# One output tile stored row by row through a single transfer, five stores cut in two: attention, then a channel mix

## The chip, the core and the metric

The kernel runs on one core of a Trainium2 chip. The core has a matmul engine (TensorE, PE in the profile; PEld is its loading of weights), a vector engine (VectorE, DVE), an activation engine (ScalarE, ACT), GpSimd (POOL) and SyncE (SP). Each engine runs its own list of instructions in order, and engines wait for each other by semaphores. Data move between memory (HBM) and the on-chip buffer (SBUF) by DMA; SP, ACT and POOL can issue transfers. Matmul results land in eight PSUM banks. The metric is the device time of one execution in microseconds (us).

## The reference

The first half is an attention through 32 memory slots for 8 batches, 8 heads, 576 tokens and head width 64; the second is a channel mix over the result, `x` of 8 x 576 tokens and 512 features:

```python
a = softmax(phi)                      # over the 32 slots
k_m, v_m = a^T k, a^T v               # per batch and head
x = softmax(q k_m^T / 8) v_m          # -> x[b, s, 512]
x_prev = x moved on by one token, zero at s = 0
xk = mu_k * x + (1 - mu_k) * x_prev   # and xr with mu_r
out = sigmoid(xr w_r) * (max(xk w_k, 0)^2 w_v)
```

`w_k` is 512 x 1024, `w_v` 1024 x 512, `w_r` 512 x 512. The output is float32, 8 x 576 rows of 512.

## The kernel before

**Tokens in blocks of 64.** A batch's 576 tokens are taken as 64 rows p by NJ = 9 positions j, token = 9p + j, and are kept in the order j first (from batch 1 on with j = 0 last): a block is the 64 tokens of one j. In this order the previous token's block is simply the block before. An output tile t is 128 places, that is two blocks of 64; there are 36 tiles. One block's rows lie nine rows apart in the output. Two neighbouring blocks j and j + 1 of one batch are, for each p, two adjacent rows in the output.

**Stages.** Per batch, attention steps give normalised weights (`atn`) and slot values (`vb`). From batch 1 on the rest goes by chunks of 512 places: chunk step `x8:v` makes x for chunk 8 with matmuls, `x8:d0d` and `x8:d2d` the difference to the token before (two feature blocks of 128 each), and the four mixes `x8:k0d`, `x8:k2d`, `x8:r0d`, `x8:r2d` scale the difference by mu (line 563) and add x (line 568), which writes xk or xr into a ring. The ring `xkT` (and `xrT`) is 128 partitions x 4 feature blocks x 2304 columns, bf16; a place's column is its number modulo 2304. The last block of each batch is written by an add of its own (line 572).

**What reads the rings.** A key step such as `c7:3` (chunk 7, hidden block 3) does four matmuls over the four feature blocks of `xkT` (line 611), then a relu on ACT (line 615) and a square on ACT or DVE (lines 621, 623) into `sq`. A gate step `g:28` (tile 28) does four matmuls from `xrT` (line 644) and a tanh on ACT (line 647). A value step `o:31` does eight matmuls from `sq` (line 665); DVE combines them with the gate into one of four `o` buffers (line 673) and the rows are stored. For the last four tiles a value step can be cut into halves of 256 columns: `o:33b` and `o:33a`.

**What sets the order.** Nothing is scheduled: the order is written out by hand in the strings of `PLAN`, and every engine gets its instructions in that order. The layer below places the semaphore waits from what each instruction reads and writes. Around the change the plan reads

```python
"c6:5 7:y1 g:26 x7:vm g:25 g:27 x7:d0d x7:d2d x7:k0d x7:r2e x8:v o:24 x7:k2d o:25 o:26 o:27 x8:d0d x7:r0e c7:1",
"c7:6s x8:d2d x8:k0d c7:3s c7:7s g:29 x8:k2d c7:5 c7:4 g:31 c8:1 c8:5s c7:0 c7:2 g:30 x8:r0d c8:0s c8:4 c8:2",
"x8:r2d o:31 c8:7 g:28 c8:3s g:32 c8:6s o:28 o:30 g:35 g:33 o:29 o:32 o:33b g:34 o:35 o:34 o:33a",
```

Chunk 7 is places 3648 to 4159, ring columns 1344 to 1855; chunk 8 is places 4160 to 4607, columns 1856 to 2303.

**Stores.** Each tile is stored by two transfers, one for each block of 64 rows (line 599): both from SP, but for the last four tiles the second block from ACT. A transfer raises one of eight completion counts; SP's and ACT's transfers take the eight in turn, in the order in which they are written. At the end of the program SP passes one wait for each count, in a fixed order, before the engines meet and the execution ends.

Of the kernel before, what the change touches and what calls it, by code (L numbers as in the profile page):

```python
# [53 lines left out]

NJ = 9
SG = 4
RL = 3
HALF_ROOT = 0.5 ** 0.5

# [2 lines left out]
def kernel(  # L62
# [13 lines left out]
    nc = tc.nc  # L76
    B, H, S, D = q.shape
# [8 lines left out]
    QR = S // NJ  # L86
# [15 lines left out]
    def bank():  # L102
        return f"ps{next(banks)}"
# [96 lines left out]
    for g in range(4):  # L200
        r = slice(g * M, (g + 1) * M)
# [34 lines left out]
    def turn(name, n):  # L236
        turns[name] = turns.get(name, -1) + 1
        return f"{name}{turns[name] % n}"
# [3 lines left out]
    def head_tiles(pss, st, src, lo, hi, cols=slice(0, None), **flags):  # L242
        for c in range(2):
            for g in range(HH):
                r = slice(g * M, (g + 1) * M)
                nc.tensor.matmul(pss[g][c * D:(c + 1) * D, cols], lhsT=src[r, c], rhs=st["at"][r, c, lo:hi],  # L246
                                 skip_group_check=True, **flags)
# [264 lines left out]
    def chunk_x(c):  # L512

        lo = (c - 1) * CT
        hi = min(lo + CT, TOK)
        n, plain = hi - lo, min(hi, TOK - QR) - lo
        ends = [b * S - QR for b in range(1, B) if lo <= b * S - QR < hi]

        def tile_x():
            if c not in xs:  # L520
                xs[c] = work.tile([128, ND, QR + CT], BF16, name="x", tag=f"x{c % 3}")
            return xs[c]

        def values(c0, c1, both=False):

            def go():
                x = tile_x()
                if c > 1:
                    nc.vector.tensor_copy(x[:, :, :QR], xs[c - 1][:, :, CT:])
                pss = [psum.tile([128, CT], F32, name="nops", tag=bank())[:, :c1 - c0] for _ in range(ND)]  # L530
                for b in range(1, B):
                    g0, g1 = max(lo + c0, (b - 1) * S), min(lo + c1, b * S)
                    if g0 < g1:
                        head_tiles(pss, states[b], states[b]["vb"], g0 - (b - 1) * S, g1 - (b - 1) * S,
                                   slice(g0 - lo - c0, g1 - lo - c0), start=True, stop=True)
                for i in range(ND):
                    (nc.vector.tensor_copy if both and i % 2 else nc.scalar.copy)(x[:, i, c0:c1], pss[i])  # L537
            return go

        def diff(pr, m):  # L540

            def go():
                if c not in ds:
                    ds[c] = work.tile([128, ND, CT], BF16, name="diff", tag=f"diff{c % 2}")
                x, d = xs[c][:, pr:pr + m], ds[c][:, pr:pr + m]
                nc.vector.tensor_sub(d[:, :, :plain], x[:, :, QR:QR + plain], x[:, :, :plain])  # L546
                for e in ends:
                    e -= lo
                    first = xs[c - 1][:, pr:pr + m, e:e + QR]
                    nc.vector.tensor_sub(d[:, :, e + 1:e + QR], first[:, :, 1:], x[:, :, e:e + QR - 1])  # L550
                    nc.vector.tensor_copy(d[:, :, e:e + 1], first[:, :, :1])  # L551
            return go

        def mix(which, pr, m, by_act=False):
            def go():
                ring = (xk_T, xr_T)[which][:, pr:pr + m]
                t = work.tile([128, 2, CT], BF16, name="mu_d", tag=turn("mu_d", 2))[:, :m]
                for i in range(m):
                    o = which * ND + pr + i
                    if by_act:  # L560
                        nc.scalar.activation(t[:, i, :n], ds[c][:, pr + i, :n], AF.Copy, scale=mu1[:, o:o + 1])  # L561
                    else:
                        nc.vector.tensor_scalar_mul(t[:, i, :n], ds[c][:, pr + i, :n], mu1[:, o:o + 1])
                x = xs[c][:, pr:pr + m]
                cut = -(S + lo) % RING
                for p0, p1 in ((0, cut), (cut, plain)) if 0 < cut < plain else ((0, plain),):
                    g = (S + lo + p0) % RING
                    nc.vector.tensor_add(ring[:, :, g:g + p1 - p0], x[:, :, QR + p0:QR + p1], t[:, :, p0:p1])  # L568
                for e in ends:
                    e -= lo  # L570
                    g = (S + lo + e) % RING
                    nc.vector.tensor_add(ring[:, :, g:g + QR], xs[c - 1][:, pr:pr + m, e:e + QR], t[:, :, e:e + QR])
            return go
        return values, diff, mix
# [17 lines left out]


    def store(o, t, cols):
        for n in range(2):
            b, r = divmod(t * 128 + n * QR, S)
            j = (r // QR + 1) % NJ if b else r // QR
            eng = nc.scalar if n and t >= NTOK // 128 - 4 else nc.sync
            eng.dma_start(out=out[b].rearrange("(p j) d -> p j d", j=NJ)[:, j, cols], in_=o[n * QR:(n + 1) * QR, cols])

    def keys(c):
        start = STARTS[c]
# [2 lines left out]
        def key(fi, lo, hi, by_act=False):  # L605
            def go():
                pk = psum.tile([128, CT], F32, name="pk", tag=bank())[:, :hi - lo]
                cut = min(hi, -(lo + 1) // RING * -RING)
                for p0, p1 in ((lo, cut), (cut, hi)) if cut < hi else ((lo, hi),):
                    for di in range(ND):  # L610
                        nc.tensor.matmul(pk[:, p0 - lo:p1 - lo], lhsT=wk_sb[:, di, fi * 128:(fi + 1) * 128],  # L611
                                         rhs=xk_T[:, di, p0 % RING:p0 % RING + p1 - p0],
                                         start=(di == 0), stop=(di == ND - 1))
                rl = work.tile([128, CT], BF16, name="rl", tag=turn("rl", RL))[:, :hi - lo]
                nc.scalar.activation(rl, pk, AF.Relu, scale=HALF_ROOT)  # L615
# [15 lines left out]
    gated, outs, homes, parts = {}, {}, {}, {}  # L631
    free = {"sg": list(range(SG)), "o": list(range(4))}

# [18 lines left out]
    def value(t, hs=((0, 1),), n=1, f0=0, f1=NF):  # L652

        def go():
            p = t * 128 % (2 * S)
            for h0, h1 in hs:
                cols = slice(h0 * Dm // n, h1 * Dm // n)
                pv = opened.get(t) if f1 - f0 < NF else None
                fresh = pv is None
                if fresh:  # L660
                    pv = psum.tile([128, Dm], F32, name="pv", tag=bank())
                if f1 - f0 < NF:
                    opened[t] = pv
                for fi in range(f0, f1):
                    nc.tensor.matmul(pv[:, cols], lhsT=sq[:, fi, p:p + 128], rhs=wv_sb[:, fi, cols],  # L665
                                     start=(fi == 0 and fresh), stop=(fi == NF - 1),
                                     skip_group_check=f1 - f0 < NF)
                if f1 < NF:
                    continue
                if t not in outs:  # L670
                    outs[t] = take("o", t)
                o = outs[t]
                nc.vector.scalar_tensor_tensor(o[:, cols], in0=gated[t][:, cols], scalar=1.0, in1=pv[:, cols],  # L673
                                               op0=AL.add, op1=AL.mult)
                store(o, t, cols)
                parts[t] = parts.get(t, 0) + Dm * (h1 - h0) // n
            if parts.get(t) == Dm:
                for name in free:
                    free[name].append(homes[name, t])
        return go  # L680
# [19 lines left out]
    for n, word in enumerate(" ".join(PLAN).split()):  # L700
        who, _, name = word.partition(":")
# [40 lines left out]
```

## Time and profile before

| | us |
|---|---|
| median of 3 runs | 200.18 (199.85 to 200.54) |
| the profiled execution, its own time | 199.63 |
| its span, first to last instruction | 197.9 |
| PE busy | 189.6 (96%) |
| DVE busy | 158.3 (80%) |
| ACT busy | 146.9 (74%) |
| POOL busy | 31.0 (16%) |
| mean granted TensorE clock, share of full | 0.988 |

The profile is of one execution, and times in it count from the start of its span. A row of the timeline gives the start, the busy time, the engine, the line of the kernel, the operation, out<-in, the shapes and how many such instructions it merges; in square brackets stands how long the engine was idle before and what ended that. The chain of waits follows the work that ended last back from the end; in order of time each row is start, length, engine, tile and line. A row of a group gives the count, the busy time, the mean of one in ns and the idle time before. A window's row gives the busy time of each engine in it, the granted clock (PEclk; 1.00 is full) and the DMA share.

### The profile page before, as it was taken

What the parts mean: (1) busy time and instruction counts of PE and PEld (TensorE: products, weight loads), DVE (VectorE), ACT (ScalarE), POOL (GpSimd) and SP (SyncE); (2) the same over time, 40 slices, a digit from 0 to 9 for tenths busy, and PEclk for the clock granted to TensorE, in tenths of its full rate; (3) what the DMA queues carried; (4) which work ended last, traced back from release to release, by engine and by line L of the source; (5) the groups of instructions that cost most, each with busy time, mean ns of one, the idle gap of its engine ahead of it and who ended that gap; (6) DMA issues with size and microseconds to landing.
All of it is one profiled execution on the core that took longest, in us unless ns stands there. A gap on an engine that the chain in (4) does not pass through costs nothing.

```text
span 197.9 us, 5488 instructions
## 1 busy us (share of the span) xinstructions
PE 189.6 (96%) x2182; PEld 96.7 (49%) x2205; DVE 158.3 (80%) x440; ACT 146.9 (74%) x302; POOL 31.0 (16%) x47
## 2 busy tenths in 40 slices
PE   7988999999999999999999999999999999999991
PEld 2534665765454445445357645444443444444550
DVE  6079869899979998999999999999996997452232
ACT  2338779696989998899998978897699759854210
POOL 7824333412040040004700000000000000000000
PEclk9979999999999999999999999999999999999998
DMA  6999999999999999955999953232240063012444
GB/s 164 189 263 212 205 207 198 266 224 279 239 280 228 221 304 205 215 117 151 217 234 279 251 101 79 57 83 53 66 96 3 2 146 68 0 29 48 98 123 130
DMA packets 24554, 31.30 MB, mean 158 GB/s; under 512 B 1992, under 2 KB 19664, under 8 KB 24528
## 3 DMA queue, kind: packets, MB, share of 16 engines
q0 software_dynamic: 17424, 20.91, 56.6%
q1 hardware_dynamic: 6176, 8.92, 17.9%
q10 hardware_dynamic: 928, 1.11, 1.7%
q8 instruction: 17, 0.28, 0.6%
q14 instruction: 9, 0.07, 0.1%
HBM read 38.28 MB, written 9.44 MB: 241 GB/s over the span
## 4 chain that ended last, share of the span: by engine, by line
PE 82%; DMA 9%; POOL 4%; ACT 1%; issue 1%; DVE 1%; POOLq 0%
PE pk L611 30%; PE pv L665 30%; PE pr L644 16%; DMA wk<-in_moe_w_k_dram 9%; PE kvps L280 4%; PE nops L246 2%; PE scps L372 1%; POOL q L183 1%; POOL kvs L126 1%; ACT x L537 1%; ACT mu_d L561 1%; POOL kvs L129 1%; POOL ph L122 0%; POOL wk L167 0%; DVE diff L546 0%
## 5 line engine op out<-in xcount | busy, mean ns | idle before, releaser
L611 PE MATMUL pk<-xkT,wk 128*128 128x512 bf16 (+4 forms) x345 | 67.5, 340 | 0.6 <-DMA wk<-in_moe_w_k_dram 0.2
L665 PE MATMUL pv<-wv,sq 128*128 128x512 bf16 (+1 forms) x321 | 65.6, 353 | 0.3
L615 ACT ACTIVATE rl<-pk 128x512 bf16<-128x512 f32 (+3 forms) x80 | 42.9, 554 | 10.9 <-PE pk L611 10.3
L611 PEld LDWEIGHTS <-wk 128*128 128x128 bf16 x352 | 33.0, 98 | 28.5 <-issue 1.1
L665 PEld LDWEIGHTS <-sq 128*128 128x128 bf16 x328 | 31.3, 98 | 30.0 <-issue 0.8
L644 PE MATMUL pr<-wr,xrT 128*128 128x512 bf16 x135 | 34.7, 379 | 0.6 <-issue 0.2
L673 DVE SCALAR_TENSOR_TENSOR o<-sg,pv 128x512 f32<-128x512 f32 (+1 forms) x41 | 24.3, 613 | 13.3 <-PE pv L665 12.2
L647 ACT ACTIVATE sg<-pr 128x512 f32<-128x512 f32 x36 | 20.9, 601 | 9.7 <-PE pr L644 9.5
L561 ACT ACTIVATE mu_d<-diff,mu 128x512 bf16<-128x512 bf16 x34 | 22.4, 717 | 3.6 <-DVE diff L551 2.1
L623 DVE TENSOR_TENSOR sq<-rl 128x192 bf16<-128x192 bf16 (+5 forms) x66 | 18.9, 319 | 7.7 <-ACT rl L615 7.0
L644 PEld LDWEIGHTS <-xrT 128*128 128x128 bf16 x144 | 13.5, 98 | 15.5 <-issue 0.7
L621 ACT ACTIVATE sq<-rl 128x512 bf16<-128x512 bf16 (+5 forms) x38 | 19.8, 535 | 1.0
L537 ACT CAST x<-nops 128x512 bf16<-128x512 f32 (+3 forms) x32 | 15.1, 560 | 4.0 <-PE nops L246 4.0
L357 DVE STREAM_TRANSPOSE qT<-q 128x576 uint32<-128x576 uint32 x16 | 11.8, 755 | 2.3 <-DMA q<-in_q_dram 2.3
L432 DVE TENSOR_TENSOR atn<-e,lz 128x256 bf16<-128x256 bf16 (+1 forms) x32 | 13.0, 445 | 0.1
L377 ACT ACTIVATE e<-scps 128x288 bf16<-128x288 f32 x32 | 10.5, 416 | 3.4 <-PE scps L372 3.4
L546 DVE TENSOR_TENSOR diff<-x 128x1024 bf16<-128x1024 bf16 (+1 forms) x16 | 10.7, 671 | 1.9 <-ACT x L537 1.6
L423 DVE STREAM_TRANSPOSE lz<-se 128x256 f32<-128x256 f32 (+2 forms) x24 | 12.0, 527 | 0.1
L216 PE MATMUL idle<-zeros 128*128 128x512 bf16 (+1 forms) x35 | 10.7, 466 | 1.0 <-DVE zeros L144 1.0
L414 DVE TENSOR_REDUCE se<-eT 128x18 f32<-128x576 bf16 (+3 forms) x17 | 11.2, 659 | 0.2
L266 ACT ACTIVATE em<-ph 128x1152 bf16<-128x1152 f32 (+1 forms) x9 | 9.4, 1053 | 2.6 <-DMA ph<-in_phi_dram 2.6
L568 DVE TENSOR_TENSOR xrT<-x,mu_d 128x1024 bf16<-128x1024 bf16 (+3 forms) x18 | 10.9, 613 | 0.5 <-ACT mu_d L561 0.2
(72 smaller groups left out, 152.6 us busy)
## 6 DMA issues: line engine op xcount, KB each, us to landing
out_dram<-o SPq DMA_DIRECT2D x59, 128.0 KB, 2.4
kvs<-in_v_dram POOLq DMA_DIRECT2D x8, 576.0 KB, 14.2
ph<-in_phi_dram POOLq DMA_DIRECT2D x7, 576.0 KB, 13.1
kvs<-in_k_dram POOLq DMA_DIRECT2D x7, 576.0 KB, 15.8
q<-in_q_dram POOLq DMA_DIRECT2D x6, 576.0 KB, 16.8
q<-in_q_dram POOLq DMA_DIRECT2D x4, 288.0 KB, 10.4
out_dram<-o SPq DMA_DIRECT2D x18, 64.0 KB, 5.3
wk<-in_moe_w_k_dram POOLq DMA_DIRECT2D x2, 512.0 KB, 15.2
```

The source lines that it names most:

```text
L423: nc.vector.transpose(st["lz"].rearrange("p c (b t h) -> p (c b) h t", t=PB, h=2)[:, b0:b0 + n], st["se"][:, b0:b0 + n].unsqueeze(3).to_br ...
L432: nc.vector.tensor_mul(st["at"][:, c, sl], st["e"][:, c, sl], st["lz"][:, c, sl])
L537: (nc.vector.tensor_copy if both and i % 2 else nc.scalar.copy)(x[:, i, c0:c1], pss[i])
L561: nc.scalar.activation(t[:, i, :n], ds[c][:, pr + i, :n], AF.Copy, scale=mu1[:, o:o + 1])
L611: nc.tensor.matmul(pk[:, p0 - lo:p1 - lo], lhsT=wk_sb[:, di, fi * 128:(fi + 1) * 128], rhs=xk_T[:, di, p0 % RING:p0 % RING + p1 - p0], sta ...
L615: nc.scalar.activation(rl, pk, AF.Relu, scale=HALF_ROOT)
L621: nc.scalar.activation(sq[:, fi, p:p + p1 - p0], rl[:, part], AF.Square)
L623: nc.vector.tensor_mul(sq[:, fi, p:p + p1 - p0], rl[:, part], rl[:, part])
L644: nc.tensor.matmul(pr, lhsT=xr_T[:, di, c0:c0 + 128], rhs=wr_sb[:, di, :], start=(di == 0), stop=(di == ND - 1))
L647: nc.scalar.activation(gated[t], pr, AF.Tanh, scale=0.5)
L665: nc.tensor.matmul(pv[:, cols], lhsT=sq[:, fi, p:p + 128], rhs=wv_sb[:, fi, cols], start=(fi == 0 and fresh), stop=(fi == NF - 1), skip_gr ...
L673: nc.vector.scalar_tensor_tensor(o[:, cols], in0=gated[t][:, cols], scalar=1.0, in1=pv[:, cols], op0=AL.add, op1=AL.mult)
```

## The change

Tile 33 is places 4224 to 4351, ring columns 1920 to 2047, two neighbouring blocks of one batch. The changed kernel keeps these 128 places in another order: the two blocks are interleaved, so that place 2p + n of the tile holds row p of block n. All mixes that write these columns are cut in three adds: the 64 columns before the tile, the tile's 128 with a step of two columns in the write, and the 192 after. Only chunk 8 has them, so four mixes are touched. Everything that follows works on the tile's places in whatever order they stand; only the store must know it. It becomes, for each half of the columns, one transfer of 128 rows from SP, in place of one of 64 rows from SP and one of 64 from ACT. Apart from that, for tiles 20, 22, 23, 25 and 26 the first block's transfer is cut into two of 256 columns each, both from SP.

```diff
+SPLIT = (20, 22, 23, 25, 26)
+PAIRED = 33
...
                 cut = -(S + lo) % RING
-                for p0, p1 in ((0, cut), (cut, plain)) if 0 < cut < plain else ((0, plain),):
+                pair = PAIRED * 128 - S - lo
+                pieces = ((0, cut), (cut, plain)) if 0 < cut < plain else ((0, plain),)
+                if 0 < pair < plain:
+                    pieces = ((0, pair), (pair, pair + 128), (pair + 128, plain))
+                for p0, p1 in pieces:
                     g = (S + lo + p0) % RING
-                    nc.vector.tensor_add(ring[:, :, g:g + p1 - p0], x[:, :, QR + p0:QR + p1], t[:, :, p0:p1])
+                    to, a0, a1 = ring[:, :, g:g + p1 - p0], x[:, :, QR + p0:QR + p1], t[:, :, p0:p1]
+                    if p0 == pair:
+                        to = to.rearrange("k c (p n) -> k c n p", n=2)
+                        a0, a1 = (a.rearrange("k c (n p) -> k c n p", n=2) for a in (a0, a1))
+                    nc.vector.tensor_add(to, a0, a1)
...
     def store(o, t, cols):
-        for n in range(2):
-            b, r = divmod(t * 128 + n * QR, S)
-            j = (r // QR + 1) % NJ if b else r // QR
+        at = [(b, (r // QR + 1) % NJ if b else r // QR) for b, r in
+              (divmod(t * 128 + n * QR, S) for n in range(2))]
+        if t == PAIRED:
+            (b, j), _ = at
+            nc.sync.dma_start(out=out[b].rearrange("(p j) d -> p j d", j=NJ)[:, j:j + 2, cols], in_=o[:, cols])
+            return
+        for n, (b, j) in enumerate(at):
             eng = nc.scalar if n and t >= NTOK // 128 - 4 else nc.sync
-            eng.dma_start(out=out[b].rearrange("(p j) d -> p j d", j=NJ)[:, j, cols], in_=o[n * QR:(n + 1) * QR, cols])
+            mid = (cols.start + cols.stop) // 2
+            for c in (slice(cols.start, mid), slice(mid, cols.stop)) if t in SPLIT and n == 0 else (cols,):
+                eng.dma_start(out=out[b].rearrange("(p j) d -> p j d", j=NJ)[:, j, c], in_=o[n * QR:(n + 1) * QR, c])
```

## The prediction

> **What bounds the kernel now.** I read the head of the page and the chain of waits, then the chain in order of time and the timeline where the change acts, then the last microseconds.
>
> ```profile
> span 197.9 us, 5488 instructions
> PE 189.6 (96%) x2182; PEld 96.7 (49%) x2205; DVE 158.3 (80%) x440; ACT 146.9 (74%) x302; POOL 31.0 (16%) x47
> PE 82%; DMA 9%; POOL 4%; ACT 1%; issue 1%; DVE 1%; POOLq 0%
> ```
> ```profile
> 157.96 1.94 PE pv L665 x9
> 159.90 3.45 PE pk L611 x16
> 163.35 0.86 PE pr L644 x4
> 164.21 1.08 PE pk L611 x5
> ...
> 166.80 3.24 PE pk L611 x16
> ...
> 177.28 0.86 PE pr L644 x4
> ...
> 193.61 0.02 issue
> 193.63 0.42 DVE o L673
> ```
>
> TensorE (PE) is the bound: from 157.96 to 193.61 the chain is matmuls without a hole but for a few 0.05 us of issue. Whatever stops PE here moves the end by as much; what VectorE (DVE) and SyncE (SP) do costs nothing until PE waits for it. The changed adds stand in this stretch:
>
> ```profile
> 159.74 3.62 PE L611 MATMUL pk<-xkT,wk 128*128 128x512 bf16 x16
> 162.55 0.42 DVE L623 TENSOR_TENSOR sq<-rl 128x512 bf16<-128x512 bf16 x1
> 162.88 0.55 DVE L546 TENSOR_TENSOR diff<-x 128x768 bf16<-128x768 bf16 x1
> 163.56 0.57 DVE L563 TENSOR_SCALAR mu_d<-diff,mu 128x448 bf16<-128x448 bf16 x2
> 164.17 0.56 DVE L568 TENSOR_TENSOR xkT<-x,mu_d 128x768 bf16<-128x768 bf16 x1
> 164.64 0.22 DVE L572 TENSOR_TENSOR xkT<-x,mu_d 128x128 bf16<-128x128 bf16 x1
> 164.78 0.57 DVE L563 TENSOR_SCALAR mu_d<-diff,mu 128x448 bf16<-128x448 bf16 x2
> 165.39 0.56 DVE L568 TENSOR_TENSOR xkT<-x,mu_d 128x768 bf16<-128x768 bf16 x1
> 165.86 0.22 DVE L572 TENSOR_TENSOR xkT<-x,mu_d 128x128 bf16<-128x128 bf16 x1
> ```
>
> The 16 matmuls from 159.74 are the steps c7:1, c7:6, c7:3, c7:7, four each, 3.45/16 = 0.216 us apart; the 164.17 add is x8:k0d, the 165.39 add x8:k2d. PE is some 2.7 us ahead of DVE here (c7:3's first at 159.74 + 8 x 0.216 = 161.47): c7:3 and c7:7 come after x8:k0d in the written order, yet they are issued before x8:k0d's add begins, because they read chunk 7 and it writes chunk 8.
>
> **Part 1: the interleaved add puts a wait into PE's path.** Tile 33 is ring columns 1920 to 2047, all in chunk 8. Each of the four x8 mixes now does three adds (64, 128 interleaved, 192 columns) for one of 384. In the built program of the changed kernel the order on every engine is the old one, but two matmuls and two adds have gained a wait:
>
> ```
> -L627 Matmult pk<-xkT,wk 128x512
> +L627 Matmult pk<-xkT,wk 128x512 [waits DVE_49]
>  ...
> +L578 TensorTensor xkT<-x,mu_d 128x2x2x64 [waits PE_49]
> ```
>
> The matmuls are the second of c7:3 (feature block 1) and the fourth of c7:5 (block 3). Followed by the counts, they wait for the interleaved add of x8:k0d and of x8:k2d. The adds wait for reads of block 1 in c7:6 and of block 3 in c7:7. None shares an element with the other: c7 reads columns 1344 to 1855. But a partition's blocks lie 2304 columns apart, and from column 1920 of block 0 to 2047 of block 1 the interleaved write reaches across columns 1344 to 1855 of block 1; the layer that places the waits does not tell them apart. On xrT no such wait appears.
>
> What it costs. The second matmul of c7:3 is the tenth of the 16: 159.74 + 9 x 0.216 = 161.68. The add it now waits for ends after x8:k0d's first piece (128 elements a partition; the step from 164.64 to 164.78 gives 0.14) and its own duration, which the trace does not show. The nearest rows for 256 elements:
>
> ```profile
> L623 DVE TENSOR_TENSOR sq<-rl 128x256 bf16<-128x256 bf16 x6 | 1.7, 285 | 0.4 <-ACT rl L615 0.2
> L432 DVE TENSOR_TENSOR atn<-e,lz 128x256 bf16<-128x256 bf16 x16 | 6.5, 409 | 0.0
> ```
>
> The first is packed bf16 throughout, the second has an f32 input; 0.29 to 0.41 us, and I take 0.41, as this add too is not packed in all its operands. The Trainium skill, "VectorE: DVE Perf Modes", Mode 2x_1P, gives two elements a cycle only to a step of one, which would make the dearer end right; at the other end the sum would be 0.12 us less, and no run here shows which. So the add ends at 164.17 + 0.14 + 0.29 to 0.41 = 164.60 to 164.72, and PE sees it 0.04 later (DVE's last row ends at 193.63 + 0.42 = 194.05, SP's store that waits for it starts at 194.09, below). PE stands still from 161.68 to 164.64 or 164.76: 2.96 to 3.08 us, **taken as 3.0**. DVE does not get there sooner: in the windows it is busy 3.38 of 3.41 and 3.31 of 3.41 us (below), and before that point it waits for nothing that PE does later.
>
> The second wait is then late for nobody. c7:7 ends near 163.35 + 3.0 = 166.35; x8:k2d's interleaved add, ready near 165.39 + 0.2 (k0d's extra adds) + 0.14 = 165.7, waits until 166.4 and ends by 166.8. PE reaches the fourth matmul of c7:5 at 164.21 - 0.16 + 3 x 0.216 + 3.0 = 167.7, 0.9 later (the chain's times run 0.16 behind the issue, 159.90 to 159.74). Step c8:1 comes 3.0 after its 166.80. Nothing after it waits longer: each x8:r mix grows by some 0.15 to 0.3 us (a step of 0.47 for 768 elements, 164.17 to 164.64, becomes by the same slope 0.14 + 0.21 to 0.33 + 0.27), x8:r0d ahead of an idle 1.02 us on DVE, x8:r2d ending near 175.7 for a gate that PE starts at 177.28.
>
> ```profile
> 173.38 0.83 DVE L623 TENSOR_TENSOR sq<-rl 128x448 bf16<-128x448 bf16 x2 [1.02 <-ACT rl L615]
> ...
> 175.21 0.22 DVE L572 TENSOR_TENSOR xrT<-x,mu_d 128x128 bf16<-128x128 bf16 x1
> ```
>
> **Part 2: what the clock does with 3 us of standstill.** The granted clock changes on a grid of 3.41 us (5.24, 8.65, 12.06, ...):
>
> ```profile
> core 0: us, PE busy (x) PEld busy (x) DVE busy (x) ACT busy (x) POOL busy (x), PEclk, DMA share, GB/s
> 8.65:12.06 3.41, 2.66 (x52) 1.57 (x43) 1.79 (x5) 0.99 (x3) 1.76 (x3) 1.00 1.19 199
> 12.06:15.47 3.41, 3.41 (x85) 1.29 (x74) 2.72 (x6) 1.85 (x6) 0.24 (x2) 0.50 1.15 292
> 15.48:18.89 3.41, 2.79 (x86) 1.39 (x78) 3.18 (x11) 2.79 (x6) 1.31 (x2) 1.00 1.22 208
> 192.97:196.38 3.41, 0.63 (x6) 0.31 (x4) 0.95 (x2) 0.00 (x0) 0.00 (x0) 1.00 0.67 186
> 196.38:197.85 1.47, 0.00 (x0) 0.00 (x0) 0.00 (x0) 0.00 (x0) 0.00 (x0) 0.50 0.00 0
> 158.84:162.25 3.41, 3.41 (x17) 1.57 (x16) 3.38 (x9) 1.19 (x2) 0.00 (x0) 1.00 0.67 153
> 162.25:165.66 3.41, 3.36 (x17) 1.57 (x16) 3.31 (x13) 3.31 (x8) 0.00 (x0) 1.00 0.70 157
> ```
>
> A window with 0.63 us of matmuls was followed by half clock, and so was one with 2.66 us of mostly small ones; 2.79 us of somewhat fuller ones kept the clock. With the standstill at 161.7 to 164.7 the window 162.25 to 165.66 keeps 3.41 - 2.45 = 0.96 us of matmuls, nearer to the 0.63 than to any that kept the clock. A window at half clock does 1.7 us less work; where the grid cuts the standstill later, 1.3. **I take 1.5 us, at a little over even odds**, since the grid need not lie the same in each execution and a cut through the middle would leave 1.9 us in each window. The Trainium skill, "TensorE: Matmul & The Clock Gate", Why this matters for your kernels, speaks against this: it allows idle gaps up to about 3 us, by which the clock would hold and 202.8 be right, case (a). The trace agrees with its window of 3.4 us but not that a whole window must be idle (0.63 and 2.66 us above).
>
> **Part 3: tile 33's store and the end.** The last add's rows went out by two stores, SP's and ACT's; now one on SP.
>
> ```profile
> 193.63 0.42 DVE L673 SCALAR_TENSOR_TENSOR o<-sg,pv 128x256 f32<-128x256 f32 x1
> 194.09 0.55 SPq L599 DMA_DIRECT2D out_dram<-o  x1
> 194.13 0.80 ACTq L599 DMA_DIRECT2D out_dram<-o  x1
> DMA to landing us min/median/max: 2.3/2.4/2.6
> L737 SPq EVENT_SEMAPHORE  x5: 28/28/28, 196.7 to 197.0; - x5
> ```
>
> SP's half lands at 194.09 + 2.3 = 196.4, ACT's at 194.13 + 2.6 = 196.7. One store of twice the rows lands between these: gain 0 to 0.3 us, 0.15 taken. Then SP passes its closing waits one by one: five from 196.7 to 197.0, (197.0 - 196.7)/4 = some 0.07 us each, because ACT's store counted on the fifth of the list from the end. In the changed build three stores more have been issued by then (five added, two saved), the eight completion counts have turned by three, and the last store counts on the one waited for last: four steps, 0.25 us. **The end gains 0.25 to 0.55, 0.4 taken.**
>
> **Part 4: the five split stores.** Each is one SP store more, 0.57 us and a gap, at 136 to 163 us:
>
> ```profile
> L599 SPq DMA_DIRECT2D out_dram<-o x16: 466/566/605, 136.1 to 163.0; - x16
> ...
> DMA to landing us min/median/max: 2.2/2.4/2.6
> ```
> ```profile
> 176.05 18.59 SPq L599 DMA_DIRECT2D out_dram<-o  x13
> ```
>
> SP has no store between 163.6 and 176.05, so tiles 25 and 26 push tile 27's store back by 1.3 us at most, landed by 168; DVE writes no output tile before it is through with x8:r2d, after 175.2 (above). Without that gap they would cost 1.3 us. Taken as 0, DVE's extra wait instructions too: it runs them ahead.
>
> **The sum** on the profiled execution: 199.63 + 3.0 + 1.5 - 0.4 = 203.7. It is 0.55 under the median of 200.18, whose sum is 204.3; I say 204.2, as the runs spread by 0.7.
>
> **Rivals.**
> (a) The clock holds: only the standstill counts, 200.18 + 3.0 - 0.4 = 202.8. For it: a grid line near the middle of the standstill. Against: the 0.96 us that the profile's grid leaves.
> (b) Not slower: the wait is met before PE comes to it, and only the end's gain is left, 199.8. It decides at 161.64: x8:k0d's interleaved add would have to end 3 us earlier. DVE has 0.13 us idle in the two windows before, so there is no room.
> (c) The second wait stalls too: the interleaved add takes over 1.2 us. What is beyond it costs PE twice; an add of 2 us stalls it 4.7 and 0.85 us, some 207 with the slower clock. Against: the 0.41 row.
>
> **How the numbers follow.** Forecast 0.53, (a) 0.39, (b) 0.04, (c) 0.04. The range 202.1 to 204.9 holds the first two, from the clock that holds on a run 0.5 below the median, with 0.1 more at the end, to 3.1 + 1.7 - 0.25 on the median and 0.2 of spread; the forecast's own range is 203.6 to 204.9. A change under 0.3%, 0.6 us, can't be told from none here: slower 0.96, same 0.03 (case b), faster 0.01.
>
> **What would show it.** A PE idle of 3 us put down to DVE's xkT add after the second c7:3 matmul, near 161.7; x8:k2d's interleaved add idle before it, waiting for PE; a granted clock of 0.5 for one window near 165.7 if the forecast is right, 1.0 if (a) is; chain rows after 165 shifted by 3.0 or 4.5; the end after the last add shorter by 0.4. No idle at 161.7 would make all of it wrong but Part 3.

## The result

The changed kernel takes 203.21 us, the median of five executions (202.59 to 203.28); the kernel before takes 200.40 beside it (199.85 to 200.54). The ratio is 1.014, 95% interval 1.012 to 1.016: slower by 2.8 us. The profiled execution took 202.62 us, with a span of 200.85 against 197.85.

The head of the page of the changed kernel:

```profile
span 200.8 us, 5501 instructions
PE 190.5 (95%) x2182; PEld 97.0 (48%) x2205; DVE 159.3 (79%) x448; ACT 147.1 (73%) x302; POOL 31.0 (15%) x47
```

The page counts the same 2182 matmuls on PE, in about the same busy time (189.6 us before). So the 3 us are no added work on PE; they are time in which it stands still. The timeline of PE and DVE around chunk 8's first mix (start, busy time, engine, line, operation, shapes; in brackets the idle time before and what ended it):

```profile
159.96 2.11 PE L627 MATMUL pk<-xkT,wk 128*128 128x512 bf16 x9
...
163.82 0.57 DVE L565 TENSOR_SCALAR mu_d<-diff,mu 128x448 bf16<-128x448 bf16 x2
164.43 0.83 DVE L578 TENSOR_TENSOR xkT<-x,mu_d 128x128 bf16<-128x128 bf16 x3
165.07 1.67 PE L627 MATMUL pk<-xkT,wk 128*128 128x512 bf16 x7 [3.00 <-DVE xkT L578]
...
165.92 0.23 DVE L578 TENSOR_TENSOR xkT<-x,mu_d 128x128 bf16<-128x128 bf16 x1
166.57 1.03 PE L660 MATMUL pr<-wr,xrT 128*128 128x512 bf16 x4
166.77 0.69 DVE L578 TENSOR_TENSOR xkT<-x,mu_d 128x256 bf16<-128x256 bf16 x2 [0.62 <-PE pk L627]
...
167.44 1.89 PE L627 MATMUL pk<-xkT,wk 128*128 128x512 bf16 x7
```

Before, the row of c7:1, c7:6, c7:3 and c7:7 held sixteen matmuls without a hole. Now it breaks after nine: PE has done four of c7:1, four of c7:6 and one of c7:3, and the tenth, due at 159.96 + 9 x 0.216 = 161.90, is issued at 165.07, when DVE's add of x8:k0d is through. That is 3.17 us late by its start. Later DVE's second interleaved add waits 0.62 us for c7:7. The matmul of c7:5 that waits for that add is the fourth of the row from 167.44, due at 167.44 + 3 x 0.216 = 168.09; it is not held up, since no idle time stands at that row. The two interleaved adds in the groups of DVE between 164 and 168 us (count, busy time, mean ns of one, idle before):

```profile
L578 DVE TENSOR_TENSOR xkT<-x,mu_d 128x256 bf16<-128x256 bf16 x2 | 0.9, 446 | 0.6 <-PE pk L627 0.6
L578 DVE TENSOR_TENSOR xkT<-x,mu_d 128x384 bf16<-128x384 bf16 x2 | 0.7, 350 | 0.0
```

One of 256 elements takes 446 ns, longer than one of 384 elements that is not interleaved.

The end: the chain's last row, the row of the paired store, its landing (the three stores issued from 196.9 on), and SP's closing wait that is left once it has landed:

```profile
197.02 0.42 DVE o L689
```
```profile
197.48 0.57 SPq L609 DMA_DIRECT2D out_dram<-o  x1
```
```profile
DMA to landing us min/median/max: 2.5/2.6/2.7
```
```profile
L753 SPq EVENT_SEMAPHORE  x1: 28/28/28, 199.9 to 199.9; - x1
```

From the end of the last add (197.44) to the end of the span (200.85) it is 3.41 us; before it was 3.80 (194.05 to 197.85). The paired store lands 2.45 us after its issue, and one closing wait is passed after it, where five were.

So the span of the profiled execution grew by 3.00: 3.17 at the tenth matmul, 0.22 that c7:1 already began later (159.96 for 159.74), less 0.40 at the end. The granted clock has no part in these 3 us: no window at the standstill or behind it ran at half clock. The windows, cut at the lines of its own clock grid (columns: length, then busy time and count of PE, PEld, DVE, ACT, POOL, then PEclk, DMA share, GB/s):

```profile
159.94:163.35 3.41, 2.12 (x10) 0.88 (x9) 3.38 (x10) 1.82 (x3) 0.00 (x0) 1.00 0.50 114
163.35:166.76 3.41, 1.69 (x8) 0.77 (x8) 2.73 (x12) 0.82 (x2) 0.00 (x0) 1.00 0.67 148
166.76:170.18 3.42, 3.37 (x16) 1.57 (x16) 1.44 (x5) 3.10 (x6) 0.00 (x0) 1.00 0.00 0
```

A grid line at 163.35 cuts the standstill near its middle, 2.12 and 1.69 us of matmuls are left on its two sides, and the clock stays full: rival (a), with its condition.

### The profile page after: what moved, and what is told of

It reads as the page before. It is cut to its first block, busy times and chain, and to the rows that moved or that the text cites. A ratio compares the mean times of both kernels' runs of the same rounds, so it can differ in the third digit from the quotient of the medians.

```text
span 200.8 us, 5501 instructions
## 1 busy us (share of the span) xinstructions
PE 190.5 (95%) x2182; PEld 97.0 (48%) x2205; DVE 159.3 (79%) x448; ACT 147.1 (73%) x302; POOL 31.0 (15%) x47
## 4 chain that ended last, share of the span: by engine, by line
PE 73%; DMA 8%; DVE 7%; ACT 4%; POOL 3%; issue 3%; DVEq 0%; POOLq 0%
PE pk L627 26%; PE pv L681 26%; PE pr L660 14%; DMA kvs<-in_k_dram 8%; PE kvps L282 4%; ACT rl L631 2%; PE scps L374 1%; DVE diff L548 1%; DVE xkT L578 1%; ACT mu_d L563 1%; DVE o L689 1%; PE nops L248 1%; POOL q L185 1%; DVE mu_d L565 1%; ACT x L539 1%
## 5 line engine op out<-in xcount | busy, mean ns | idle before, releaser
L218 PE MATMUL idle<-zeros 128*128 128x512 bf16 (+1 forms) x35 | 11.4, 489 | 1.0 <-DVE zeros L146 1.0
L578 DVE TENSOR_TENSOR xkT<-x,mu_d 128x1024 bf16<-128x1024 bf16 (+4 forms) x22 | 11.4, 537 | 1.0 <-PE pk L627 0.6
L578 DVE TENSOR_TENSOR xrT<-x,mu_d 128x1024 bf16<-128x1024 bf16 (+4 forms) x22 | 11.4, 544 | 0.5 <-ACT mu_d L563 0.2
```

Source lines behind the costliest of these rows:

```text
L578: nc.vector.tensor_add(to, a0, a1)
```

## Experiments: the wait

**The interleaved add made block by block.** The changed kernel, but each interleaved add is made as one add for each feature block. Every write then stays within one block of the ring, and what is computed is the same.

```diff
                     if p0 == pair:
                         to = to.rearrange("k c (p n) -> k c n p", n=2)
                         a0, a1 = (a.rearrange("k c (n p) -> k c n p", n=2) for a in (a0, a1))
+                        for i in range(m):
+                            nc.vector.tensor_add(to[:, i], a0[:, i], a1[:, i])
+                        continue
                     nc.vector.tensor_add(to, a0, a1)
```

> The changed kernel with one edit: the interleaved add of tile 33's 128 columns is made as two adds, one for each feature block, of the same elements with the same step of two columns; in the built program no matmul and no add then has the extra wait. Theory (the 3 us come from the wait that the layer places for a write reaching over a whole feature block): PE's idle of 3.0 us before the second matmul of c7:3 is gone, c7:3 runs ahead of the x8:k0d add as before the change, and only the end's gain of 0.43 us is left: 200.4 - 0.4 = 200.0, the last add's end to the end of the span 3.36 us. Rival (the step of two columns itself, or the longer DVE list, holds PE up): DVE has one instruction more per mix than the changed kernel, so the stall stays, 203 or more.

Measured: 199.31 us against 199.79 of the kernel before, ratio 0.998, interval 0.996 to 0.9997. The timeline there:

```profile
160.10 3.62 PE L630 MATMUL pk<-xkT,wk 128*128 128x512 bf16 x16
163.56 1.03 PE L663 MATMUL pr<-wr,xrT 128*128 128x512 bf16 x4
...
164.58 0.23 DVE L581 TENSOR_TENSOR xkT<-x,mu_d 128x128 bf16<-128x128 bf16 x1
164.72 0.50 DVE L579 TENSOR_TENSOR xkT<-x,mu_d 128x128 bf16<-128x128 bf16 x2
```

The sixteen matmuls run without a hole again, long before the same elements are written at 164.72. So they never needed that data, and the wait was a false one. The two adds even take 0.50 us together, more than the one of 0.44: it is not DVE's time that cost 3 us but whom its writes are taken to concern. So the rival of the expectation, that the step of two columns or the longer list on DVE holds PE up, is out. This version is faster than both kernels, if only by some 0.5 us than the kernel before (0.1 to 0.8 by the interval): the loss is gone, and the 0.4 us of the end stays.

**The interleaved adds alone.** The stores are those of before, so the 128 rows of tile 33 stand in each other's places in the output.

```diff
-SPLIT = (20, 22, 23, 25, 26)
+SPLIT = ()
...
-        if t == PAIRED:
+        if False:
```

> The kernel before with the interleaved adds of the four x8 mixes and nothing else: the stores are those of the kernel before, so that tile 33's rows land in each other's places (its 128 output rows are wrong). Theory: the whole loss, and none of the end's gain: 200.4 + 3.2 = 203.6, PE idle 3.0 us before c7:3's second matmul, the end as before at 3.80 us after the last add. Rival (the stores have part in the loss): less than 203.2, with a shorter idle.

Measured: 205.41, 203.13, 205.52 and 202.95 us, ratio 1.022 (1.017 to 1.027), beside 199.79 of the kernel before. One group at 3.2 us over before was expected; there are two, 2.4 us apart, and only the lower is that one (203.0, 3.2 over). The profiled execution is the first, of the upper group. Its windows at its own grid lines:

```profile
163.39:166.81 3.42, 1.09 (x6) 0.49 (x6) 3.35 (x14) 0.70 (x2) 0.00 (x0) 1.00 0.66 144
166.81:170.22 3.41, 3.41 (x10) 1.21 (x9) 0.83 (x3) 2.81 (x5) 0.00 (x0) 0.50 0.00 0
170.22:173.63 3.41, 3.36 (x17) 1.65 (x17) 0.85 (x2) 2.03 (x4) 0.00 (x0) 1.00 0.00 0
```

Here most of the standstill falls into one window, 1.09 us of matmuls are left in it, and the next window runs at half clock: ten matmuls in the time of seventeen. This is the drop that the prediction put at 1.5 us and that the profiled execution of the result does not show. Here it costs 3.41 / 2 = 1.7 us. It is not the whole distance of the two groups: in this execution c7:1 also began at 160.66, 0.9 later than in the profile of the kernel before (159.74).

## Experiments: the stores

**The split stores alone** (no tile is kept interleaved, so the mixes and the last stores are those of before):

```diff
-PAIRED = 33
+PAIRED = 99
```

> The kernel before with the five stores cut in two and nothing else. Theory (the five only turn the eight completion counts on by five): PE and DVE as before; the stores of the last add then count on the first two of the closing waits in place of the fourth and fifth, so that after the last landing seven waits follow in place of four: 3 x 0.06 = 0.2 us later, 200.6, the last add's end to the end of the span 4.0 us. Rival (the extra stores hold up tiles 24 to 27 or the transfers beside them): a DVE wait for an out store, 201 or more. Third: no effect at all, 200.4.

**Block by block, without the split stores**, so with the paired store but one store less for each of the five tiles:

```diff
-SPLIT = (20, 22, 23, 25, 26)
+SPLIT = ()
```

> As the two-adds kernel, without the five split stores. Theory (the split stores are worth what they turn the counts by): the last store counts on the third of the eight, five closing waits follow its landing in place of none: 0.30 us more than with the split stores, 200.3, the last add's end to the end of the span 3.66 us. Rival (the counts are worth nothing; one transfer for two is the whole gain): as the two-adds kernel, 200.0.

Measured: 200.13 us for the split stores alone (ratio 1.0015, 0.9997 to 1.0032) and 199.63 for the paired store without them (0.9988, 0.9972 to 1.0004). Alone each makes no difference that can be told from none; together, in the block-by-block kernel, they gain. The closing waits of SP that begin after the last landing show why (count, duration in ns, first and last start), first for the split stores alone, then for the paired store alone:

```profile
L753 SPq EVENT_SEMAPHORE  x8: 28/28/28, 197.4 to 197.8; - x8
```
```profile
L756 SPq EVENT_SEMAPHORE  x6: 28/28/28, 197.1 to 197.4; - x6
```

The one released by the last landing is among them, so seven and five more follow, where the changed kernel has none. Each costs some 0.06 us ((197.358 - 197.055) / 5). From the last add to the end it is 3.97 us with the split stores alone (4.0 expected), 3.71 with the paired store alone (3.66 expected), and 3.40 with both block by block (3.36 expected), for 3.80 before. The five extra stores do nothing where they stand; they turn the completion counts, so that the last store counts on the wait that comes last. In the kernel with both this is worth 0.31 us of the 0.40 (3.71 - 3.40), and the paired store by itself, one closing wait more than before included, 0.09 (3.80 - 3.71).

## Experiments: the clock

**The changed kernel again**, on another chip:

> The changed kernel once more, for how often the clock drops. The same standstill of 3.1 us at the second matmul of c7:3 in each execution; only where the 3.41-us grid cuts it differs. Theory: half clock follows a window with 2 us or more of standstill, so a cut near the middle (about 1.0 to 2.0 us of its length, a third or so of all phases) holds the clock, the others drop it. Then two groups of times: 2.8 us over before (some 202.8 on a before of 200.0), and 4.5 to 5.3 us over it (some 204.9), neither empty, as with the interleaved adds alone (203.0 and 205.4). Rival: only a window without any matmul drops it; a standstill of 3.1 us never empties a window of 3.41, so there is one group, 2.8 us over before, and the 205.4 of the interleaved adds alone had another cause.

**The add made later.** The two scalings ahead of x8:k0d's adds are repeated, with the same values, four times in one kernel and eight times in another:

```diff
-                        nc.vector.tensor_scalar_mul(t[:, i, :n], ds[c][:, pr + i, :n], mu1[:, o:o + 1])
+                        for _ in range(4 if (c, which, pr) == (8, 0, 0) else 1):
+                            nc.vector.tensor_scalar_mul(t[:, i, :n], ds[c][:, pr + i, :n], mu1[:, o:o + 1])
```

> The add that PE waits for is made 1.5 us later: the two scalings of x8:k0d are made four times over, the same values each time. A scaling is 0.25 us after the one before it, six more are 1.48 us, so the standstill at c7:3 is 3.17 + 1.48 = 4.65 us. With the clock held the time is 1.5 us over the changed kernel's lower group, 204.3 on a before of 200.0. Theory (2 us of standstill in one window is enough): wherever the grid cuts 4.65 us, one of the windows has 2.3 us or more of it, so the clock always drops and the time is 205.6 to 206.7, no execution near 204.3. Rival (only a wholly empty window drops it): 4.65 - 3.41 = 1.24 us of phases in 3.41, a third of the executions drop and two thirds stay at 204.3.

> The same with the two scalings made eight times over: 14 more by 0.25 us, 3.45 us, a standstill of 6.6 us. With the clock held 3.45 us over the changed kernel's lower group, 206.3 on a before of 200.0. Both theories drop the clock in nearly all executions here (6.6 us empties a window in 94 of 100 phases), but a part of the half-clock window lies in the standstill itself: 206.3 plus 0.1 to 2.4, and a window of 0.5 is expected in the profile within 3.41 us after the first emptied window.

**Work put ahead of the wait**, by the order of the plan alone:

```diff
-    "c7:6s x8:d2d x8:k0d c7:3s c7:7s g:29 x8:k2d c7:5 c7:4 g:31 c8:1 c8:5s c7:0 c7:2 g:30 x8:r0d c8:0s c8:4 c8:2",
+    "c7:6s x8:d2d x8:k0d g:29 g:31 c7:3s c7:7s g:30 x8:k2d c7:5 c7:4 c8:1 c8:5s c7:0 c7:2 x8:r0d c8:0s c8:4 c8:2",
```

> The changed kernel with the order of three gate steps moved: g:29 and g:31 go ahead of c7:3, g:30 to where g:29 was. PE then has two gate steps, 2 x 0.86 us, to do before it comes to the wait: the standstill falls from 3.17 to 1.44 us and the time by 1.73 against the changed kernel's lower group: 1.1 us over before, some 201.1 on a before of 200.0. Less than 2 us of standstill in any window: the clock holds in all phases, so one group of times. If PE's lead is not what is lost (the adds delay something else), the time stays at the changed kernel's.

Measured, beside 199.90 us of the kernel before: the changed kernel 204.53 (204.03 to 205.43, six executions; ratio 1.022, 1.019 to 1.025); four times 207.25 (206.80 to 207.54); eight times 210.05 (209.39 to 211.00); the gates ahead 200.65 (1.0038, 1.0018 to 1.0057).

On this chip no execution of the changed kernel was in the lower group, 202.8. The expectation had both groups filled, so it missed there; its rival, one group at 202.8, is out as well. The row of PE with the standstill in the profiled execution, 205.43 us, and then its windows:

```profile
164.89 3.15 PE L627 MATMUL pk<-xkT,wk 128*128 128x512 bf16 x7 [2.99 <-DVE xkT L578]
```
```profile
160.67:164.08 3.41, 1.23 (x6) 0.48 (x5) 3.38 (x12) 1.82 (x3) 0.00 (x0) 1.00 0.52 117
164.08:167.50 3.42, 2.61 (x7) 0.96 (x7) 1.82 (x8) 1.10 (x2) 0.00 (x0) 0.50 0.52 116
167.50:170.91 3.41, 3.41 (x10) 1.21 (x9) 0.83 (x3) 1.95 (x4) 0.00 (x0) 0.50 0.00 0
170.91:174.32 3.41, 3.41 (x18) 1.62 (x17) 0.85 (x2) 2.29 (x4) 0.00 (x0) 1.00 0.00 0
```

The same kernel and the same standstill, but the grid line comes at 164.08, near the standstill's end. A window is left with 1.23 us, and two windows at half clock follow. They lose half of their busy time, (2.61 + 3.41) / 2 = 3.0 us; the span is 2.8 longer than that of the profile in the result (203.7 for 200.8), and c7:1 began 0.16 earlier.

The scalings repeated behave as the theory has it: by their times all eight executions drop (two of them were profiled). Their standstills came out longer than worked out (5.2 and 8.2 us for 4.65 and 6.6), because a scaling that writes where the one before it wrote starts 0.37 us after it, not 0.25. With the measured standstills the lower groups would lie near 202.7 + 2.2 = 204.9 and 202.7 + 5.2 = 207.9; the lowest executions are 206.80 and 209.39. The rival, that only an empty window drops the clock, would have left about half of the executions with four scalings near 204.9, as 5.2 us empties a window in (5.2 - 3.41) / 3.41 of the phases. And in the profile of that kernel no window is empty, yet the clock drops; first its windows, then those of the kernel with eight:

```profile
161.45:164.86 3.41, 0.81 (x4) 0.29 (x3) 3.31 (x13) 1.59 (x3) 0.00 (x0) 1.00 0.56 125
164.86:168.28 3.42, 0.80 (x2) 0.25 (x2) 3.24 (x12) 0.00 (x0) 0.00 (x0) 0.50 0.48 105
168.28:171.69 3.41, 3.41 (x9) 1.18 (x8) 1.08 (x5) 2.22 (x4) 0.00 (x0) 0.50 0.00 0
```

```profile
162.62:166.03 3.41, 0.00 (x0) 0.00 (x0) 3.23 (x11) 0.91 (x2) 0.00 (x0) 1.00 0.69 150
166.03:169.44 3.41, 0.00 (x0) 0.00 (x0) 3.09 (x11) 0.00 (x0) 0.00 (x0) 0.50 0.21 48
169.44:172.86 3.42, 2.18 (x6) 0.81 (x6) 2.22 (x9) 0.68 (x2) 0.00 (x0) 0.50 0.00 0
172.86:176.27 3.41, 3.41 (x10) 1.21 (x9) 0.83 (x3) 2.37 (x4) 0.00 (x0) 0.50 0.00 0
176.27:179.68 3.41, 3.41 (x18) 1.62 (x17) 0.85 (x2) 2.07 (x4) 0.00 (x0) 1.00 0.00 0
```

A half-clock window with 2.18 us of matmuls is followed by another, one filled with 3.41 is not.

With the gates ahead, PE has other work first:

```profile
159.58 1.89 PE L627 MATMUL pk<-xkT,wk 128*128 128x512 bf16 x8
162.31 1.90 PE L660 MATMUL pr<-wr,xrT 128*128 128x512 bf16 x8 [0.84 <-DVE xrT L578]
164.05 0.38 PE L627 MATMUL pk<-xkT,wk 128*128 128x512 bf16 x1
164.68 1.67 PE L627 MATMUL pk<-xkT,wk 128*128 128x512 bf16 x7 [0.26 <-DVE xkT L578]
```

The wait at c7:3 shrinks to 0.26 us, and the gates meet one of 0.84 of their own, a true one, for xr of chunk 7, which the expectation had not seen. It only takes part of the same time: the second matmul of c7:3, the eighteenth from 159.58, is due at 159.58 + 17 x 0.216 = 163.25 and issued at 164.68, 1.43 late for 1.44 expected. The kernel is 0.75 us over before, by the interval 0.4 to 1.1, for 1.1 expected. So the loss is PE's lead over DVE and shrinks by the work that is put ahead; what is left still costs more than the end gains.

**Once more, with a shorter standstill beside it**, on a third chip. First the changed kernel, then the plan with x8:k0d ahead of x8:d2d, then the interleaved adds alone as above:

> The changed kernel on another chip. So far five executions of it lay 2.8 us over before and six 4.1 to 5.5 us over it; the traces fit this: a window of the 3.41-us grid in which matmuls do less than somewhere between 1.3 and 1.7 us of work at full clock is followed by one at half clock (1.22 us of work was, 1.69 was not), and a half-clock window that begins with the rest of the standstill is followed by another. With a standstill of 3.1 us and a limit of 1.5 us of work (1.9 us of standstill), the cuts that hold the clock are 1.2 to 1.9 us into it: 0.7 us of 3.41, one phase in five. Theory: most executions at 4.1 to 5.5 us over before, few or none at 2.8; if the phase stays the same for all executions on a chip, all of one kind. Rival (a chip drops the clock or does not, whatever the phase): the profile would show a cut that leaves under 1.3 us of work and no half clock after it, or one that leaves over 1.7 in both windows and half clock.

```diff
-    "c7:6s x8:d2d x8:k0d c7:3s c7:7s g:29 x8:k2d c7:5 c7:4 g:31 c8:1 c8:5s c7:0 c7:2 g:30 x8:r0d c8:0s c8:4 c8:2",
+    "c7:6s x8:k0d x8:d2d c7:3s c7:7s g:29 x8:k2d c7:5 c7:4 g:31 c8:1 c8:5s c7:0 c7:2 g:30 x8:r0d c8:0s c8:4 c8:2",
```

> The changed kernel with x8:k0d written ahead of x8:d2d. On DVE the three instructions of x8:d2d (163.15 to 163.82 in the changed kernel's trace, 0.67 us) then come after the add that PE waits for: the standstill falls by 0.67 us, to 2.4 to 2.5 us. With the clock held the time is 0.67 us under the changed kernel's lower group, 2.1 us over before. By the limit of 1.9 us of standstill in a window the cuts that hold are 0.6 to 1.9 us into it, 1.3 of 3.41, two phases in five; the others cost 1.2 to 2.5 us more, so two groups, 2.1 and 3.3 to 4.6 us over before, the lower one now with a good part of the executions. If DVE's place in its list is not what sets the standstill, nothing moves.

> The interleaved adds alone once more (the stores of before, so that the 128 rows of tile 33 stand in each other's places in the output), beside the changed kernel on the same chip. The same standstill, without the 0.4 us that the changed kernel gains at the end: each of its groups is 0.4 us over the changed kernel's, 3.2 us over before where the clock holds and 4.5 to 5.9 us where it drops, in the same shares as the changed kernel has them here.

Measured, beside 199.81 us of before: the changed kernel 203.81 (1.020, 1.017 to 1.022), one execution at 202.76 and five from 203.78 to 204.41; x8:k0d first 202.05 (201.29 to 202.51; 1.010, 1.008 to 1.013); the interleaved adds alone 203.25 (202.49, 202.89, 203.60, 204.90). The windows of the changed kernel's profiled execution, 203.82 us, and then of the interleaved adds alone, 202.49 us:

```profile
161.00:164.41 3.41, 0.81 (x4) 0.29 (x3) 3.34 (x14) 1.60 (x3) 0.00 (x0) 1.00 0.55 125
164.41:167.82 3.41, 3.00 (x8) 1.04 (x8) 1.47 (x7) 1.23 (x2) 0.00 (x0) 0.50 0.48 106
167.82:171.24 3.42, 3.37 (x16) 1.55 (x16) 1.28 (x5) 2.89 (x5) 0.00 (x0) 1.00 0.00 0
```
```profile
159.65:163.06 3.41, 1.93 (x9) 0.78 (x8) 3.38 (x9) 1.82 (x3) 0.00 (x0) 1.00 0.72 159
163.06:166.48 3.42, 1.94 (x10) 0.88 (x10) 2.73 (x13) 1.06 (x2) 0.00 (x0) 1.00 0.41 91
```

In the first, one window at half clock follows and costs 3.00 / 2 = 1.5 us, the very size of the prediction's term: its time is 1.2 over that of the profiled execution in the result, and its c7:1 began 0.25 earlier. In the second the cut is in the middle and the clock holds, as it did in the profile of the result. So whether it drops goes by where the grid cuts the standstill, and not by the chip alone: the third has both kinds, by these two profiles and, by the times, for one and the same kernel. The execution at 203.60 fits neither group of the expectation; no trace of it shows why.

With x8:k0d first the standstill is 0.67 us shorter, as expected, 2.33 for 3.00:

```profile
164.61 1.67 PE L627 MATMUL pk<-xkT,wk 128*128 128x512 bf16 x7 [2.33 <-DVE xkT L578]
```

In its windows the grid cuts the standstill in the middle, and the clock holds:

```profile
160.01:163.43 3.42, 2.27 (x11) 0.93 (x10) 3.38 (x10) 1.82 (x3) 0.00 (x0) 1.00 0.51 117
163.43:166.84 3.41, 2.23 (x11) 1.05 (x11) 3.31 (x15) 1.35 (x3) 0.00 (x0) 1.00 0.71 156
```

The median, 2.24 us over before, is that of the lower group (2.1 expected). But two executions in five were expected there, and by their times all six are. Part of the miss is the limit: 1.9 us of standstill in a window was taken for it, and the traces allow up to 2.1 (below), which makes it one in two. Six of six is still more than that.

## Why the prediction came out as it did

**Part 1, right.** The wait, its place and nearly its size: PE is idle for 3.00 us before the second matmul of c7:3. The prediction counted from the start at which that matmul was due, and had 2.96 to 3.08; counted so, it is 3.17. Of the 0.09 beyond the upper end, 0.04 is DVE's own lateness against PE, 0.03 the interleaved add (0.44 for 0.41) and the rest the way from DVE to PE. The dearer of the two rows for the add was the nearer. The second wait was late for nobody, and nothing after it waited longer. The block-by-block kernel shows that this wait is the whole of the loss.

**Part 2: the drop of the clock exists, but it did not come in the executions of the result; this is the step that failed.** The term of 1.5 us for the clock measured nothing in the five executions at 202.59 to 203.28; they are rival (a), 2.8 over before, where its sum had 2.6 (202.8 for 200.18). The range held the result because it was drawn around both cases. In the two later sets of the same kernel the time over before was 4.6 and 4.0, where the forecast had 4.0. The prediction laid the grid of the profile before over the changed kernel, found 0.96 us of matmuls left in a window, and allowed that the grid need not lie so. In the profile of the result it did not: the line at 163.35 left 2.12 and 1.69. What the prediction lacked was the limit, which its rows left wide open (0.63 us dropped and 2.79 held, but 2.66 us of smaller matmuls dropped too), and that a second window can follow at half clock, which makes the drop cost up to 3.0 us, not 1.7, and takes single executions over the range's upper end (205.43 for 204.9).

The limit, from the windows shown (us of matmuls in a window of 3.41):

| clock in the window | then half clock | then full clock |
|---|---|---|
| full | 0.00, 0.81, 1.09, 1.23 | 1.69, 1.93, 1.94 |
| half | 0.00, 0.80, 2.18, 2.61 | 3.00, 3.41 |

Halved, as what a window at half clock does in work at full clock, the lower row is 0.00, 0.40, 1.09, 1.31 and 1.50, 1.70. So one limit, between 1.31 and 1.50 us of work at full clock, fits every one of them; a single limit of busy time does not, since 2.61 dropped and 1.69 held. Two limits of busy time, one for each state of the clock, would fit as well, and no run here tells the two readings apart. Nor does the limit carry over to the first 24 us, where the matmuls are smaller: there 2.95 us of them were followed by half clock (with the gates ahead, 9.02 to 12.44) and 2.04 us were not (the interleaved adds alone on the third chip, 12.88 to 16.29). With a standstill of 3.1 us the clock holds if no window has more than 1.9 to 2.1 us of it: for 0.7 to 1.1 us of the 3.41 over which the cut can lie, a fifth to a third. Of the seventeen executions of the changed kernel six held by their times (three were profiled), which is not far from it, but they came in bunches: five of five, none of six, one of six. What sets the grid's place in an execution, and so why they bunch, stays open.

The Trainium skill, "TensorE: Matmul & The Clock Gate", What's actually happening, says that the window of 3413 ns runs freely and does not start over with a kernel. The traces agree: the line that cuts the standstill lay at 163.35, 164.08 and 164.41 in three executions of the same kernel. The same page of the Trainium skill, Why this matters for your kernels, allows gaps up to about 3 us and speaks of a window of idle. A gap of 2.99 us lies at the edge of the first, and the clock dropped; against the second the measurement decides, since the window before that drop held 1.23 us of matmuls.

**Part 3, right.** 0.40 us at the end, taken as 0.4: one closing wait after the last landing, and a landing between SP's and ACT's (2.45 us after issue). Four closing waits fewer at 0.06 us are 0.24 of it, and 0.16 is left for the landing, for 0.25 and 0.15 in the prediction.

**Part 4, right.** The split stores alone cost nothing that can be told from none (ratio 1.0015, an interval that holds 1); their worth is in the counts that they turn.

**Rivals.** (a) is what the executions of the result show. (b), not slower, would have needed the add 3 us earlier; the standstill shortened by 0.67 us with 0.67 us less of DVE work ahead of it shows that each microsecond on DVE there is one on PE. (c), a second wait that costs, did not come: the add takes 0.45 us, not 1.2.

## What to carry to other kernels

When a write becomes strided over several blocks of a buffer, look at which waits the built program has gained: the layer may take the write to concern everything between its first and its last element, and an engine that ran ahead then waits for data that it does not read. Splitting the write so that each instruction stays within one block removed a loss of 3 us here, for 0.06 us more on DVE. Price a standstill of PE near the length of a clock window as two cases, the clock that holds and the clock that drops, since the same kernel gave 202.6 and 205.4 us; and before choosing between them from one profile's grid, remember that the grid may lie elsewhere in the next execution.

## What the runs showed that was not expected

- One limit of work fits every clock window shown around the standstill, 1.31 to 1.50 us at full clock in 3.41, if what a half-clock window does is counted at half; that reading is not shown against one of two limits. A window at half clock with 2.61 us of matmuls was followed by another, one with 3.00 was not.
- Closing waits that find their count complete still cost SP some 0.06 us each, so which of eight counts the last store raises is worth up to seven of them, 0.4 us.
- A bf16 add with a step of two in its write took 446 ns for 256 elements a partition, more than the 350 of an add of 384 without it.
- A scaling that writes again where the one before it wrote starts 0.37 us after it, where one that writes elsewhere starts 0.25 after.
